# Other order of the recorded part, other layout of the experts' branches, few rows gathered early, the last full expert in groups of rows, and 22 unread products, in an attention–MLP–mixture-of-experts kernel

## The chip, the cores and the metric

One core of a Trainium2 chip runs the whole program. The metric is the device time of one execution in microseconds. TensorE is called PE, VectorE DVE, ScalarE ACT, GpSimd POOL and SyncE SP, as in the profile; "PEq", "SPq" and so on are the sequencers of these engines, which take the instructions in program order.

## The reference

Three blocks follow one another on 1152 tokens (two batches of 576) of width 512:

```python
# attention, 8 heads of 64, bias from the distance of two positions
x = (log1p(abs(i - j)) / log1p(max(i, 1)))[..., None]
bias = relu(x @ w1 + b1) @ w2
out = softmax(scale * q @ k.T + bias) @ v
# MLP, 512 -> 2048 -> 512
h = x @ w_in
y = (h * tanh(softplus(h))) @ w_out
# mixture of experts, top 1 of 8, capacity 288, 512 -> 1024 -> 512
e = argmax(y @ w_gate); gate = softmax(y @ w_gate)[e]
out[token] = gate * (relu(y[token] @ w1[e]) @ w2[e])   # the first 288 tokens of each expert
```

## The kernel before, in words

**The recorded part.** Attention, MLP and the routing are not written in the order in which they run. Each function records small operations (a product into one bank, an activation of one tile, one DMA) in a plan, and `emit` then walks the hand-written table `ORDER`: an entry is 8 times the number of the operation plus the number of its way, and the way picks the engine where an operation may run on more than one. The table alone sets what every engine and DMA queue finds in its row. The work goes in five tiles of 128 query rows: bias of the tile (matmuls at L518, activations at L507, a round trip of the bias row through memory, `bscr<-rbe` out and `ra<-bscr` back), scores (L619, L633), exponentials (L655), products with v (L727), then MLP in (L835) and out (L868, L872). L654 is DVE's first operation on the scores.

Matrices of the MLP and of the experts are split into a high and a low part in f16, and a product is three: high·high, high·low, low·high. L310 and L307 are DVE's and L1419 is ACT's instruction for such halves of a weight.

**The routing.** One-hot rows, counts (L1330) and slots give each expert its rows, at most 288 = 3 chunks of 96. The rows of the first expert are fetched by three indirect DMAs of POOL (L1144), split by ACT and DVE (L1149 is the low half), and turned by products with a 0/1 matrix (`first_slots`, L1173 and L1177; L1179 copies them out into `xT`). The last tile's tokens come from on-chip data; L1040 are sums of slots.

**The experts.** This part is plain code. `experts_list` sorts the experts by DVE; in this input three experts are full (`nf` = 3, more than 48 rows) and one has few rows (`nv` = 4). SP reads the sorted list into registers (L1595 to L1602), loads the next expert's first matrix (`load1`), the rows' table (`table`, L1396), and the second matrix (`load2`). `gemm1(k)` (L1434) makes 8 groups of 12 matmuls of 288 columns, `gemm2(k)` (L1467) 4 groups of 24, and behind each group transposes its result (`back`, L1453) and multiplies by the gate (L1454). `gather(k+1)` (L1402) fetches the next expert's rows and `xt` (L1424) turns them, inside `gemm2(k)`. `finish` ends with three scatters of 96 rows into `out` (L1448); in the loop it runs in the next expert's `gemm1`. The second matrix is split in `gemm1`, behind the groups 3 to 6 for k > 0 and behind 2 to 5 for the first expert.

`expert(k)` nests: `If(nf > k+1)` (L1572) the expert and the next one, `Else` (L1585) `If(nv > k+1)` `with_few(k)`, `Else` `last(k)`. All the `If` bodies of k = 0 to 6 lie first, and their `Else` bodies behind them from the innermost to the outermost, so the two conditions that end the experts' chain lead from L1572 of k = 2 over the code of four more experts to L1585. `with_few(2)` handles the last full expert together with the few rows (at most 48, in f32): loads of its matrices (`R1f`, `R2f`, L1505, L1507), `gemm1`, then the few rows' numbers and their gather (`xgf`, L1516), then `gemm2` with the few rows' products between the groups (`few_x` L1520, `few_h` L1525, `few_flip` L1533, `few_y` L1542), `finish`, the scaling of the few rows' result (L1560) and its scatter (L1561). `gemm2_last` exists in `before` too, for an input with no few rows: it makes the second product in 3 groups of 96 rows with 24 matmuls of 512 columns each, which need no transposing, and scatters each group as it is done.

Of the kernel before, what the change touches and what calls it, by code (L numbers as in the profile page):

```python
# [22 lines left out]
P = 128  # L23
# [15 lines left out]
    15464, 15472, 15480, 152, 184, 120, 128, 144, 136, 160, 168, 176, 104, 96, 112, 192, 0, 48, 200, 15488, 224, 208,  # L39
    216, 512, 56, 1328, 232, 4681, 1280, 616, 592, 608, 4672, 1416, 528, 816, 64, 673, 88, 72, 601, 648, 521, 4664,  # L40
    440, 537, 1337, 1344, 456, 449, 433, 4689, 624, 568, 544, 488, 697, 640, 689, 632, 464, 905, 656, 833, 4625, 480,
    496, 472, 825, 4433, 680, 1289, 1352, 1296, 888, 1304, 4544, 1360, 1432, 1312, 728, 4696, 664, 4425, 80, 1425,
    4561, 896, 1144, 240, 248, 1440, 840, 552, 1368, 1320, 560, 256, 576, 969, 504, 1376, 1192, 264, 1401, 4472, 777,
    1408, 584, 1160, 881, 1384, 1056, 848, 272, 864, 961, 856, 1208, 4488, 4536, 760, 1152, 704, 912, 4873, 4417, 872,
    1464, 712, 1008, 945, 4409, 4552, 4752, 1201, 952, 1216, 1392, 4568, 720, 4616, 1072, 1168, 1224, 928, 920, 753,
    4497, 4440, 736, 4609, 4857, 4601, 4481, 976, 4864, 280, 4880, 936, 8, 744, 1064, 2616, 769, 4632, 4504, 1016,
    4793, 992, 984, 4745, 784, 800, 792, 1480, 1176, 1080, 1448, 1000, 4809, 1473, 1088, 808, 1024, 2632, 4801, 4817,
    1488, 1032, 1496, 40, 1584, 1456, 4888, 1184, 4584, 1232, 4448, 4456, 4576, 1240, 2624, 1504, 1040, 1512, 1600,
    1592, 4824, 1096, 4592, 1608, 4464, 1248, 1720, 1728, 2128, 2120, 16, 1744, 1048, 4520, 4512, 1736, 4640, 1752,
    1264, 4528, 2640, 1521, 2648, 1624, 1632, 4649, 1648, 1784, 1800, 1256, 1816, 1616, 4656, 1104, 1640, 1792, 24,  # L50
    1656, 1760, 1664, 1552, 4896, 4904, 4912, 1680, 1528, 4736, 1272, 1672, 1808, 1824, 1768, 1560, 1536, 1696, 1688,
    1704, 1832, 1544, 1872, 4833, 1880, 1888, 1904, 1712, 2688, 4729, 1128, 4704, 1776, 4712, 4840, 4760, 1136, 1568,
    1976, 1984, 4848, 1840, 2000, 1896, 1920, 2656, 1912, 1112, 1936, 1952, 1864, 2760, 1992, 4776, 1944, 1928, 2008,
    1960, 2704, 1120, 2664, 2136, 2160, 2144, 2040, 2056, 2048, 2672, 2016, 288, 416, 1968, 2072, 2776, 4768, 2696,
    2232, 2024, 2080, 2064, 2680, 2088, 2712, 2168, 2152, 2032, 2256, 2264, 2192, 32, 4920, 2240, 2176, 2200, 2248,
    296, 2096, 2376, 2720, 2312, 2328, 2400, 2384, 2296, 2208, 2184, 2768, 2304, 2408, 2392, 2216, 2472, 2976, 4720,
    4784, 5456, 4944, 4936, 2448, 4928, 2336, 2728, 2992, 2784, 2432, 2416, 2480, 2272, 2496, 2985, 424, 2736, 2792,
    2280, 4960, 2440, 2488, 2288, 2504, 2512, 3000, 2552, 2568, 2424, 2536, 2744, 2456, 2520, 2800, 2752, 1576, 2320,
    2224, 2344, 2104, 2560, 1848, 2576, 4984, 2808, 4968, 2904, 4952, 3008, 1856, 2816, 4976, 4992, 2544, 2824, 2352,
    5056, 5032, 5016, 2584, 3016, 5000, 2912, 2464, 5080, 5064, 2920, 2528, 5024, 2112, 5216, 5040, 5008, 5072, 2360,  # L60
    5120, 5048, 2928, 3024, 2936, 2592, 3032, 2368, 2600, 5088, 3040, 5136, 5152, 2608, 2832, 2848, 3224, 3216, 2944,
    2952, 5144, 5128, 2960, 3408, 3616, 3416, 2840, 3624, 5240, 3232, 5160, 5224, 3312, 5232, 5248, 2968, 3048, 5272,
    5256, 5288, 2856, 3056, 3240, 5096, 2864, 3064, 3248, 3072, 7089, 2872, 2880, 3256, 3264, 3120, 3128, 5168, 3136,
    5280, 5296, 5264, 5312, 3080, 3144, 3088, 3424, 3152, 3160, 5320, 3304, 5336, 5208, 5200, 3168, 5328, 7153, 5104,
    3096, 3432, 5112, 3192, 5376, 3200, 5384, 4384, 5176, 5304, 3272, 3208, 3320, 3328, 3280, 3288, 3440, 3336, 5472,
    5496, 5480, 3448, 3456, 3512, 3520, 5568, 7105, 3344, 3464, 3296, 3352, 3472, 3360, 3368, 3392, 3400, 5504, 3528,
    5576, 5592, 5344, 5488, 3376, 10065, 3536, 5392, 5408, 5512, 3384, 5584, 5520, 3544, 7112, 5401, 3496, 312, 3552,
    376, 384, 5544, 5464, 3480, 408, 3488, 5552, 5352, 3632, 3560, 5600, 5632, 5641, 3504, 5528, 3640, 3600, 3608,
    5648, 3648, 3656, 5417, 3568, 3664, 7297, 5184, 5664, 3576, 3585, 5192, 3672, 3680, 2888, 4392, 4368, 5657, 2896,
    5673, 3832, 3824, 3105, 3720, 3728, 5360, 3177, 5369, 3592, 3689, 5536, 4376, 3736, 5424, 5432, 5712, 3704, 3696,  # L70
    5736, 5720, 7097, 7120, 7128, 5744, 7136, 5728, 3744, 3752, 5808, 5832, 3712, 5816, 7305, 3760, 5752, 3768, 7177,
    5824, 3936, 5784, 3816, 5872, 7544, 3184, 3112, 5793, 5768, 5840, 5760, 5776, 5440, 7161, 3840, 10321, 3928,
# [1588 lines left out]
```

## Time and profile before

| | us |
|---|---|
| median of 3 runs | 556.72 (555.08 to 559.42) |
| the profiled execution's own time | 556.07 |
| its span in the trace | 554.3 |
| PE busy | 492.3 (89%) |
| DVE busy | 442.0 (80%) |
| ACT busy | 389.3 (70%) |
| POOL busy | 36.6 (7%) |

The span is what the profiler recorded, first to last instruction; the execution's own time is 1.77 us longer. An engine's busy share is an average over stages: up to about 60 us the bias is made, from 60 to 415 attention and MLP run, from 415 to 431 the routing ends, and the three full experts and the few rows follow.

### The profile page before, as it was taken

To read this page: it belongs to the slowest core of one execution; us is meant where nothing else is said; L and a number is where in the kernel's file an instruction comes from. 1 tells how busy PE (TensorE), PEld (TensorE's weight loads), DVE (VectorE), ACT (ScalarE), POOL (GpSimd) and SP (SyncE) were. 2 spreads that over 40 slices of the span, in tenths; PEclk is the share of its full clock that TensorE was granted. 3 is DMA by queue.
4 is the path that set the end of the run, shared out by engine and by line. 5 is a ranking of instruction groups with operands and counts; after the bars stand their busy time and mean duration, and the time that the engine had idled before them with its cause. 6 is when DMAs were issued, how large, how long until landed. Compare 5 with 4: busy or idle time off the path is not lost.

```text
span 554.3 us, 11929 instructions
## 1 busy us (share of the span) xinstructions
PE 492.3 (89%) x4493; PEld 336.9 (61%) x4493; DVE 442.0 (80%) x1180; ACT 389.3 (70%) x803; POOL 36.6 (7%) x67
## 2 busy tenths in 40 slices
PE   5754987999999999999999999999994999977891
PEld 3311655865676754556787657995583677755460
DVE  7899999999889999999787857899878767747020
ACT  7999999989677999999876535577824377653110
POOL 1000100000000010000010000000012012202002
PEclk9786799999999999999999999999995899989797
DMA  8998775511000345257231023500002285871001
GB/s 324 381 360 300 263 279 195 209 60 60 24 2 31 133 138 195 86 178 242 81 98 38 0 83 129 178 1 2 19 23 63 89 293 153 243 284 37 8 4 43
DMA packets 28217, 73.85 MB, mean 133 GB/s; under 512 B 4838, under 2 KB 4966, under 8 KB 26096
## 3 DMA queue, kind: packets, MB, share of 16 engines
q1 hardware_dynamic: 26576, 69.21, 36.2%
q0 software_dynamic: 1568, 3.72, 2.3%
q8 instruction: 39, 0.64, 0.5%
q14 instruction: 34, 0.28, 0.2%
HBM read 55.27 MB, written 17.87 MB: 132 GB/s over the span
## 4 chain that ended last, share of the span: by engine, by line
PE 53%; DMA 16%; DVE 16%; issue 9%; ACT 4%; SPq 2%; POOL 0%; another core or an unknown queue 0%; POOLq 0%; ACTq 0%; DVEq 0%
PE pb L868 15%; PE pb L835 9%; DMA out<-OC,tid 8%; PE ps L835 5%; PE pb L727 5%; PE pb L518 4%; PE pb L663 3%; DVE rw L310 3%; DVE ra L654 3%; DMA bscr<-rbe 2%; PE ps L633 2%; PE ps L663 2%; PE pb L872 2%; ACT ra L507 1%; DVE ra L307 1%
## 5 line engine op out<-in xcount | busy, mean ns | idle before, releaser
L835 PEld LDWEIGHTS <-WIt 128*128 128x128 f16 x960 | 85.1, 98 | 9.9 <-issue 0.7
L835 PE MATMUL pb<-PX,WIt 128*128 128x256 f16 (+1 forms) x648 | 70.1, 265 | 0.0
L868 PE MATMUL pb<-WOt,ra 128*128 128x512 f16 x276 | 64.4, 379 | 0.1
L655 ACT ACTIVATE ra<-ra,rm 128x576 f32<-128x576 f32 x58 | 45.1, 779 | 10.7 <-DVE rm L654 10.3
L654 DVE CUSTOM_DVE_ANT_0 ra<-ps,ra 128x576 f32<-128x576 f32 x50 | 36.6, 752 | 9.5 <-PE ps L637 6.7
L868 PEld LDWEIGHTS <-ra 128*128 128x128 f16 x276 | 26.8, 98 | 28.1 <-issue 0.9
L507 ACT ACTIVATE ra<-AT,stab 128x320 f32<-128x320 f32 (+17 forms) x69 | 42.2, 645 | 1.5 <-DVE stab L307 1.4
L1467 PE MATMUL py<-HH,W 128*128 128x288 f16 x288 | 37.6, 286 | 1.6 <-DVE W L310 1.6
L1434 PEld LDWEIGHTS <-W 128*128 128x128 f16 x288 | 29.6, 103 | 14.0 <-issue 4.1
L727 PE MATMUL pb<-ra,AT 128*64 128x128 f32 (+1 forms) x640 | 37.0, 267 | 0.8 <-ACT ra L666 0.8
L518 PE MATMUL pb<-ra,w2s 128*32 128x512 f32 (+17 forms) x242 | 31.0, 520 | 6.0 <-ACT ra L507 3.5
L310 DVE SCALAR_TENSOR_TENSOR W<-AT,wsc,W 128x1024 f16<-128x1024 f32 x24 | 30.6, 1282 | 6.4 <-ACT W L1419 6.0
L727 PEld LDWEIGHTS pb<-ra,AT 128*64 128x64 f32 x640 | 32.1, 138 | 4.8 <-issue 2.3
L1467 PEld LDWEIGHTS <-W 128*128 128x128 f16 x288 | 28.0, 98 | 9.7 <-DVE W L310 2.2
L835 PE MATMUL ps<-PX,WIt 128*128 128x256 f16 (+1 forms) x312 | 31.1, 256 | 0.0
L310 DVE SCALAR_TENSOR_TENSOR rw<-rw 128x1024 int32<-128x1024 int32 (+1 forms) x25 | 29.8, 1195 | 0.0
L1054 POOL DMA_INDIRECT tbl<-pk,rm x9 | 10.9, 1211 | 273.3 <-DVE pk L1016 86.6
L532 ACT ACTIVATE rbe<-pb,rl 128x512 f32<-128x512 f32 (+47 forms) x57 | 25.7, 478 | 3.6 <-DMA bscr<-rbe 1.8
L619 PE MATMUL ps<-AT,rq 64*128 64x512 f32 x64 | 20.0, 703 | 8.2 <-DMA rq<-q 5.3
L663 PE MATMUL pb<-ident,ra 128*128 128x128 f32 x165 | 25.4, 283 | 1.7 <-ACT ra L655 0.9
L1434 PE MATMUL ph<-xT,W 128*128 128x288 f16 x144 | 22.4, 317 | 4.5 <-ACT jk L1206 3.9
L868 PE MATMUL pb<-WOt,rw 128*128 128x512 f16 x108 | 25.6, 379 | 0.0
(466 smaller groups left out, 1106.6 us busy)
## 6 DMA issues: line engine op xcount, KB each, us to landing
AT<-m SPq DMA_DIRECT2D x24, 512.0 KB
bscr<-rbe SPq DMA_DIRECT2D x36, 295.5 KB
ra<-bscr SPq DMA_DIRECT2D x29, 288.0 KB
rw<-wo SPq DMA_DIRECT2D x8, 1024.0 KB
rw<-wi SPq DMA_DIRECT2D x4, 1024.0 KB
WOt<-wi SPq DMA_DIRECT2D x4, 1024.0 KB
AT<-k SPq DMA_DIRECT2D x4, 576.0 KB
out<-ra SPq DMA_DIRECT2D x9, 256.0 KB
```

What stands on the lines that cost most here:

```text
L310: (eng or dve).scalar_tensor_tensor(out=out, in0=in0, scalar=s, in1=in1, op0=op0, op1=op1)
L507: on_act = lambda h_=h_, g=g: act.activation(h_.t[:, 0:dn], T[:, 0:dn], AF.Relu, bias=stab[:, g:g + 1])
L518: pe.matmul(ps.t[32 * c:32 * c + 32, 0:d1 - d0], w2s, hs[c].t[:, d0:d1], start=True, stop=True)
L532: op("ACT", c_act(n, 1, 50), lambda ends=ends: act.activation(*ends(), AF.Copy, scale=rl[:, blk:blk + 1]), r=[ps, "stab"], p=[be], alt=[(" ...
L654: op("DVE", c_dve(S), lambda i=i, own=own, m_=m_, b_=b_: dve.tensor_tensor_reduce(out=own(), in0=blk(s_.t[:, 960 * i:960 * i + S]), in1=bl ...
L655: op("ACT", c_act(S, 2), lambda i=i, m_=m_, col=col: act.activation(t_.t[:, S * i:S * i + S], t_.t[:, S * i:S * i + S], AF.Exp, bias=m_.t[ ...
L663: pe.transpose(pa.t[:, P * j:P * j + P], t_.t[:, 384 * n + P * j:384 * n + P * j + P], ident)
L727: pe.matmul(ov[64 * i:64 * i + 64, ct % 2, w * bb:w * bb + w], v_, t_.t[:, at + c0:at + c0 + w], start=n == 0, stop=n == 4)
L835: pe.matmul(ps.t[:, n * f_:n * f_ + n], WI[:, wv, ct, P * ft:P * ft + P], xt.t[:, xv, ct, 0:n], start=i == 0, stop=i == 11)
L868: pe.matmul(y_.t, gv()[:, g2, c:c + P], WO[:, wv, ft], **kw)
L1434: pe.matmul(ps[:, 0:SL], W1[:, wv, ct, P * ft:P * ft + P], XT[k % 2][:, xv, ct], start=i == 0, stop=i == 11)
L1467: pe.matmul(ps[:, 0:SL], W2[:, wv, ft, P * dt:P * dt + P], HH[:, hv, ft], start=ft == 0 and i == 0, stop=ft == 7 and i == 2)
```

## The change

Six edits. (1) `ORDER` is another permutation of nearly the same operations; it has one more. (2) That one is `unread` in `first_slots` (L1170 of the new kernel): 22 matmuls of 128x288 f16 into a bank that nobody reads, of data that are there by then, on PE in front of the first expert's row products. (3) `halves`: of the second matrix's four quarters ACT makes the high half of three, and DVE of the last; before it was two and two. (4) `gemm1` for k > 0: the row sums are reduced before the first group's low half, the size of the second matrix is found behind group 1, and its halves follow groups 2 to 5. (5) `with_few`: the few rows' gather stands before `gemm1`, `few_x` behind its seventh group, `gemm2_last` takes the place of `gemm2` and `finish`, with `few_h` and `few_flip` between its groups of rows and `few_y` at the end into another bank; the result goes to `XG[0]`, not to `OC[:, 0]`. (6) `expert`: for k below 2 as before, with the code in two functions; from k = 2 on the condition is turned, so that the end of the chain lies directly behind it and the next expert behind that.

```diff
@@ ORDER (every line differs) @@
-    15464, 15472, 15480, 152, 184, 120, 128, 144, 136, 160, 168, 176, 104, 96, 112, 192, 0, 48, 200, 15488, 224, 208,
...
+    136, 160, 104, 152, 120, 15472, 96, 128, 144, 15480, 168, 176, 112, 192, 0, 200, 184, 208, 216, 440, 888, 48, 224,
...
@@ first_slots @@
+        pz = pl.buf(RB)
+
+        def unread():
+            for i in range(22):
+                pe.matmul(pz.t[:, 0:SL], one, sl16, start=True, stop=True)
+        op("PE", 2600, unread, r=["sl1", "rc0", ("acc", 0), ("acc", 1)], w=[pz])
@@ halves @@
-        if i > 2 - m:
+        if i > 2:
@@ gemm1 @@
-            if k and ft == 2:
-                sized(k, 1, PO[0])
             act.activation(HH[:, 0, ft], ps[:, 0:SL], AF.Relu)
+            if k and ft == 0:
+                summed(k, 1)
             stt(HH[:, 1, ft], ps[:, 0:SL], 0.0, HH[:, 0, ft], ALU.max, ALU.subtract)
             if k and ft == 0:
                 finish(k - 1)
-                summed(k, 1)
-            if ft > 1 + bool(k) and ft < 6 + bool(k):
-                halves(k, 1, ft - 2 - bool(k))
+            if k and ft == 1:
+                sized(k, 1, PO[0])
+            if ft > 1 and ft < 6:
+                halves(k, 1, ft - 2)
             if k and more and ft > 3:
                 square(k + 1, 0, ft - 4, W["j"])
+            if between:
+                between(ft)
@@ gemm2_last @@
             act.activation(OC[:, c], ps, AF.Copy, scale=gat[:, c:c + 1])
             scatter(k, c)
+            if between:
+                between(c)
@@ with_few @@
         few_loads()
+        few_rows()
         if k:
-            gemm1(k, False)
-        few_rows()
-
-        def between(dt):
-            if dt == 0:
-                few_x()
-            if dt < 2:
-                few_h(dt)
-            if dt:
-                (few_flip if dt < 3 else few_y)((dt - 1) % 2)
-        gemm2(k, False, between)
-        finish(k)
+            gemm1(k, False, lambda ft: few_x() if ft == 6 else None)
+        else:
+            few_x()
+
+        def between(c):
+            if c < 2:
+                few_h(c)
+            if c:
+                few_flip(c - 1)
+        gemm2_last(k, between)
+        few_y(0)
         few_y(1)
-        act.activation(OC[:, 0], PH[0][:CS], AF.Copy, scale=sel[:, 0, 1:2])
+        act.activation(XG[0], PO[1][:CS], AF.Copy, scale=sel[:, 0, 1:2])
@@ expert @@
-        with tc.If(nf > k + 1) as more:
+        def next_():
...
-        with more.Else():
-            with tc.If(nv > k + 1) as more_:
+
+        def end():
+            with tc.If(nv > k + 1) as more:
                 with_few(k)
-            with more_.Else():
+            with more.Else():
                 last(k)
+
+        if k < 2:
+            with tc.If(nf > k + 1) as more:
+                next_()
+            with more.Else():
+                end()
+        else:
+            with tc.If(nf < k + 2) as done:
+                end()
+            with done.Else():
+                next_()
```

What stands in PE's row of instructions between the last product of the recorded attention/MLP part and the first row product of the first expert. Before (`ra_115` is the 0/1 matrix of the slots, `rw_105`, `rw_104` and `ra_109` are the high halves of the three gathered chunks):

```order
L1040 LDWEIGHTS U__150
L1040 MATMUL pb_140<-o_152,U__150 64x16
L1173 LDWEIGHTS rw_105
L1173 MATMUL pb_143<-ra_115,rw_105 128x96
L1173 LDWEIGHTS rw_104
L1173 MATMUL pb_143<-ra_115,rw_104 128x96
```

and in the changed kernel, where L1337 is the old L1330 and L1180 the old L1173:

```order
L1337 LDWEIGHTS one
L1337 MATMUL pb_144<-o_152,one 128x8
L1170 LDWEIGHTS one
L1170 MATMUL pb_142<-sl_173,one 128x288
...
L1180 LDWEIGHTS rw_106
L1180 MATMUL pb_142<-rw_105,rw_106 128x96
```

The pair at L1170 stands there 22 times, so PE passes through 22 loads and 22 products before it comes to the wait for the first expert's rows.

What stands in DVE's row at the end of the second full expert, where the chain of experts ends in this input. Before, the row behind the condition, which belongs to k = 3, and, 404 rows further on, the place to which the condition leads when it is not met:

```order
L1454 TENSOR_TENSOR OC<-po_5185,tb_5197 96x3x128
L1572 COMPARE_AND_BRANCH
L310 SCALAR_TENSOR_TENSOR HH<-ph_5181,HH 128x288
...
L1585 COMPARE_AND_BRANCH
L310 SCALAR_TENSOR_TENSOR HH<-ph_5181,HH 128x288
L1454 TENSOR_TENSOR OC<-po_5186,tb_5197 96x3x128
```

and in the changed kernel (L1606 and L1595 are the two conditions, `sel`, `tidf` and `gidf` the few rows' gate and numbers):

```order
L1465 TENSOR_TENSOR OC<-po_5219,tb_5231 96x3x128
L1606 COMPARE_AND_BRANCH
L1595 COMPARE_AND_BRANCH
L307 TENSOR_SCALAR sel<-tbf,hm 96x1 x4
L1522 TENSOR_TENSOR sel<-sel 96x2
L1523 CAST tidf<-sel 96x1
L307 TENSOR_SCALAR gidf<-sel 96x1
L327 TENSOR_REDUCE wsc<-wsc 128x1
L310 SCALAR_TENSOR_TENSOR HH<-ph_5215,HH 128x288
```

With three full experts and one of few rows both conditions now go on to the next row, and the few rows' numbers come first in it.

What stands in ACT's row from the last group of the last expert's `gemm1` to the end. Before (`YT` is a result still to be transposed, `XF`, `hs` and `HF` are the few rows):

```order
L1437 ACTIVATE HH<-pt_5188 128x288
L1468 ACTIVATE YT<-py_5183,wsc 128x288
L1521 COPY XF<-pt_5187 128x384
L1529 ACTIVATE hs<-ph_5181 96x512
L1468 ACTIVATE YT<-py_5184,wsc 128x288
L1538 COPY HF<-pt_5187 128x384
L1468 ACTIVATE YT<-py_5183,wsc 128x288
L1468 ACTIVATE YT<-py_5184,wsc 128x288
L1560 ACTIVATE OC<-ph_5181,sel 96x512
```

and in the changed kernel:

```order
L1530 COPY XF<-py_5218 128x384
L1443 ACTIVATE HH<-pt_5222 128x288
L1505 ACTIVATE OC<-py_5217,gat 96x512
L1538 ACTIVATE hs<-ph_5215 96x512
L1505 ACTIVATE OC<-py_5218,gat 96x512
L1547 COPY HF<-pt_5221 128x384
L1505 ACTIVATE OC<-po_5219,gat 96x512
L1569 ACTIVATE xg_5223<-po_5220,sel 96x512
```

The copy of the few rows has moved in front of the last group of `gemm1`, and three scaled copies that are scattered as they are take the place of four that PE still had to transpose.

## Rows read from the trace of the kernel before

**Rows 1.** The page: PE's busy tenths in 40 slices of 13.9 us

```profile
PE   5754987999999999999999999999994999977891
```

**Rows 2.** From 60 to 415: length, busy PE PEld DVE ACT POOL, PEclk, DMA share, GB/s

```profile
60.00:415.00 355.00, 347.59 (x3390) 242.36 (x3391) 314.95 (x876) 278.50 (x596) 12.89 (x32) 1.00 0.31 104
```

**Rows 3.** Chain that ended last, at 201 and at 288: start us, us, what

```profile
201.06 10.36 PE pb L868 x48
...
287.79 5.77 DMA ra<-bscr
```

**Rows 4.** PE, timeline 424 to 439: start us, us, what [idle before <-releaser]

```profile
424.98 0.34 PE L1173 MATMUL pb<-ra,rw 96*128 96x96 f16 x2 [5.33 <-DVE rw L1149]
...
430.90 5.05 PE L1434 MATMUL ph<-xT,W 128*128 128x288 f16 x24 [0.59 <-DVE xT L1179]
435.79 3.10 PE L1434 MATMUL pt<-xT,W 128*128 128x288 f16 x24
```

**Rows 5.** Two single microseconds, columns as in rows 2

```profile
418.00:419.00 1.00, 0.36 (x5) 0.26 (x5) 0.87 (x7) 0.16 (x1) 0.92 (x1) 0.50 0.46 131
...
435.00:436.00 1.00, 1.00 (x10) 0.80 (x9) 0.03 (x1) 0.01 (x1) 0.00 (x0) 1.00 0.00 0
```

**Rows 6.** Chain that ended last, at 449: the second expert's rows

```profile
448.68 6.07 DMA xg<-yscr,gid
```

**Rows 7.** PE, timeline 454 to 488

```profile
454.79 0.98 PE L1424 MATMUL pt<-ident,xg 96*128 96x96 f32 x8 [0.30 <-DMA xg<-yscr,gid]
...
459.69 1.78 PE L1434 MATMUL ph<-xT,W 128*128 128x288 f16 x12
...
472.58 2.61 PE L1467 MATMUL py<-HH,W 128*128 128x288 f16 x20
...
476.03 0.77 PE L1467 MATMUL py<-HH,W 128*128 128x288 f16 x4 [0.84 <-DVE W L310]
...
487.39 0.49 PE L1453 MATMUL po<-ident,YT 128*96 128x128 f32 x3
```

**Rows 8.** Conditions by sequencer: ns min/median/max, first to last start us

```profile
L1572 PEldq COMPARE_BRANCH  x3: 65/95/5960, 443.4 to 485.6; - x3
...
L1585 SPq COMPARE_BRANCH  x2: 34/36/38, 480.3 to 486.9; - x2
...
L1585 PEldq COMPARE_BRANCH  x2: 77/1657/3237, 491.6 to 535.8; - x2
```

**Rows 9.** DVE, timeline at 488: the last half of the last expert's first matrix

```profile
488.03 1.28 DVE L310 SCALAR_TENSOR_TENSOR W<-AT,wsc,W 128x1024 f16<-128x1024 f32 x1
```

**Rows 10.** PE, timeline 491 to 543

```profile
491.81 2.01 PE L1434 MATMUL ph<-xT,W 128*128 128x288 f16 x12 [3.93 <-ACT jk L1206]
...
505.79 2.61 PE L1467 MATMUL py<-HH,W 128*128 128x288 f16 x20
...
513.94 0.90 PE L1520 MATMUL pt<-ident,xgf 96*128 96x96 f32 x4 [3.99 <-DMA xgf<-yscr,gidf]
515.41 6.05 PE L1525 MATMUL ph<-R1f,XF 128*96 128x512 f32 x8 [0.57 <-ACT XF L1521]
...
524.56 3.60 PE L1525 MATMUL ph<-R1f,XF 128*96 128x512 f32 x8
528.00 0.49 PE L1533 MATMUL pt<-ident,hs 96*128 96x96 f32 x4
528.33 3.10 PE L1467 MATMUL py<-HH,W 128*128 128x288 f16 x24
...
538.96 3.60 PE L1542 MATMUL ph<-R2f,HF 128*96 128x512 f32 x8
```

**Rows 11.** Timelines of ACT and of POOL, from 510 to the end

```profile
542.91 0.68 ACT L1560 ACTIVATE OC<-ph,sel 96x512 f32<-96x512 f32 x1 [7.34 <-DMA out<-OC,tid]
...
510.69 0.94 POOL L1516 DMA_INDIRECT xgf<-yscr,gidf  x1 [7.02 <-DVE gidf L307]
...
549.52 0.92 POOL L1561 DMA_INDIRECT out<-OC,tidf  x1 [2.58 <-DMA out<-OC,tid]
```

More of the change, by code (lines that the diff above doesn't have):

```diff
@@ L1427, in tile_kernel, with gemm1 @@
     P3 = ((0, 0), (0, 1), (1, 0))
-    def gemm1(k, more=True):
+    def gemm1(k, more=True, between=None):
+        b_ = bool(k)
         for ft in range(8):
@@ L1454, in back, with gemm2 @@
         dve.tensor_tensor(out=OC[:, :, P * dt:P * dt + P], in0=po, in1=tb[k % 3][:, :, 1:2].bitcast(F32).to_broadcast([CS, NCH, P]), op=ALU.mult)
-    def gemm2(k, more=True, between=None):
-        if more:
-            if k == 0:
-                for i in range(4):
-                    square(1, 0, i, W["j"])
-            summed(k + 1, 0)
+    def gemm2(k):
+        if k == 0:
+            for i in range(4):
+                square(1, 0, i, W["j"])
+        summed(k + 1, 0)
         for dt in range(4):
@@ L1468, in gemm2 @@
             act.activation(YT[:, dt], ps[:, 0:SL], AF.Copy, scale=sca(k, 0, 7))
-            if more:
-                if dt == (k == 0):
-                    sized(k + 1, 0, PO[1])
-                if dt == 2:
-                    for c in range(NCH):
-                        xt(k + 1, c, (PT + PH)[c % 4])
-                if dt == 1 or dt == 2:
-                    halves(k + 1, 0, 2 * dt - 2)
-                    halves(k + 1, 0, 2 * dt - 1)
+            if dt == (k == 0):
+                sized(k + 1, 0, PO[1])
+            if dt == 2:
+                for c in range(NCH):
+                    xt(k + 1, c, (PT + PH)[c % 4])
+            if dt == 1 or dt == 2:
+                halves(k + 1, 0, 2 * dt - 2)
+                halves(k + 1, 0, 2 * dt - 1)
             if dt > 0:
                 back(k, dt - 1)
-            if more and dt > 1:
+            if dt > 1:
                 square(k + 1, 1, 2 * dt - 4, W["j"])
                 square(k + 1, 1, 2 * dt - 3, W["j"])
-            if between:
-                between(dt)
     def finish(k):
@@ L1519, in few_x @@
         for ct in range(4):
-            pe.transpose(PT[0][:, CS * ct:CS * ct + CS], xgf[:, P * ct:P * ct + P], ident[:CS, :CS])
-        act.copy(XF.rearrange("p c n -> p (c n)"), PT[0][:, 0:4 * CS])
+            pe.transpose(PY[1][:, CS * ct:CS * ct + CS], xgf[:, P * ct:P * ct + P], ident[:CS, :CS])
+        act.copy(XF.rearrange("p c n -> p (c n)"), PY[1][:, 0:4 * CS])
     def few_h(i):
```

6 lines of the change are left out of this document (3 added, 3 removed), and 216 rows, old and new, of the table ORDER.

## The prediction

> **What bounds the kernel now.** Read the page first: PE's 40 slices stand at 9 from 97 us to 416, fall to 4 in the slice from 416 to 430, and are loose from 485 to the end (7, 7, 8) [rows 1]. So there are three stages. From 60 to 415 us PE works 347.59 of 355 us at full clock [rows 2]: whatever is reordered there can win at most the 7.41 us that are left, and the chain of waits runs through PE itself, as in 48 matmuls of 512 columns in 10.36 us, 0.216 us each [rows 3]. The other two are the ones in which PE waits, and there the timeline of PE says for whom. Around 420 it stands 5.33 us, until the first expert's rows are there, and works on at half clock: the first 24 matmuls of L1434 take 5.05 us, the next 24 take 3.10 [rows 4]; in single microseconds the granted clock is 0.50 at 418 (1.2 GHz) and 1.00 (2.4 GHz) at 435 [rows 5]. From 488 on PE stands 3.93 us at the end of the experts' chain, later 0.84 and 3.99 us, and last there is a queue: POOL sends three scatters, each behind the landing of the one before, and a fourth for the few rows, at 549.52, when PE had ended at 538.96 + 3.60 = 542.56 [rows 7, 10, 11]. These are the places at which the change works.
>
> **The order of the recorded part.** The new table makes the same products. PE has 7.41 us of gaps to win from 60 to 415 [rows 2]; before 60 us it is fed by DMAs and by DVE, and the number of DVE's wide operations ahead of the first scores is nearly the same in both tables. I take 0. The bounds are about -5 us (two thirds of the gaps) and +6 us (one round trip of a bias row, 5.77 us [rows 3], that comes to stand bare).
>
> **The 22 products.** PE came to its wait at 424.98 - 5.33 = 419.65 [rows 4]. At half clock a matmul of 288 columns takes 5.05 / 24 = 0.21 us, at full clock 3.10 / 24 = 0.13. So 22 take 4.6 us if the clock is down and 2.8 if it is not: they fit into the 5.33 us and delay the rows' products by nothing, or by some tenths if PE comes later. What they can give is the clock. The row products and the first 24 of L1434 run at full clock if PE is kept busy: the 24 alone give 5.05 - 3.10 = 1.95 us, and the row products wait for copies anyhow. But PE then arrives 2 us earlier at the second expert's rows, and these do not come earlier: their gather stands on POOL behind SP's register loads and its load of the table, 448.68 + 6.07 = 454.75 [rows 6], and PE already waits 0.30 us for it [rows 7]. What the clock gives before comes back as a wait there, all but those 0.30 us, unless the lists on DVE end earlier too. I take -0.3; bounds -2.2 (the whole gain, if the lists move as well) and +2 (PE's longer wait lets the clock fall once more).
>
> **The second full expert.** The weight halves of its second matrix stand one group earlier and ACT takes one of DVE's; the stall of 0.84 us at 476.03 for the last half [rows 7] goes: -0.84. Against it, the few rows' 4 MB of weights are asked for earlier (next paragraph) and could lie on the gathers of the third expert's rows; bounds -0.84 and +0.9.
>
> **The end of the chain.** Before, PE's sequencer entered the condition at 485.6, took 5.96 us for it, and came to the next condition at 491.6; SP was through at 480.3 [rows 8]. The order shows that this is a jump over the code of four experts, and that both conditions now go on to the next row, so I take the 5.96 us away. What is late next: PE ends gemm2 at 487.88 - 0.84 - 0.3 = 486.74 [rows 7], and the last half of the first matrix ended on DVE at 488.03 + 1.28 = 489.31 [rows 9], some tenths to a microsecond earlier now. It is the eleventh of a group's 12 matmuls that needs it, 1.2 us in, so PE waits; I take 1.0 us, bounds 0.2 and 1.4. Then gemm1 takes 472.58 - 459.69 = 12.89 us as the second expert's did at full clock [rows 7], not 505.79 - 491.81 = 13.98 [rows 10], and `few_x` inside it half of its 0.90 us at half clock, 0.4. It ends at 486.74 + 1.0 + 12.89 + 0.4 = 501.0, against 505.79: -4.8, the two terms above in it. `few_x` finds its rows: the numbers are computed right behind the condition, at about 490, where the gather was issued at 510.69 before [rows 11], and 6 us later [rows 6] is 496, ahead of the seventh group's end at about 499.
>
> Here the Trainium skill has two rules. "Runtime: NRT & Kernel Launch", section Instruction fetch mechanics, says that a taken branch whose target lies outside the sequentially fetched window must fetch it before going on; the trace agrees for k = 2, with 5.96 us on PE against a median of 0.095. "Advanced Engine Details and Errata", section Control Flow Timing, gives about 108 ns for a compare-and-branch; by it the layout would be worth nothing, which this trace contradicts for a far target and bears out for the near ones (0.065 and 0.095).
>
> **The last expert's second half.** From there on, in the new order: 3 groups of 24 matmuls of 512 columns at 0.216 us, 15.5 us [rows 3]; two `few_h` and two `few_y` at 528.00 - 524.56 = 3.44 us each, 13.8 us; two flips at 528.33 - 528.00 = 0.33, 0.7 us [rows 10]. That is 30.0 us of PE without a wait: `xgf` is there, and the `few_h` that ran at half clock, 6.05 us for 3.60 [rows 10], follows no wait now. So PE ends at 531.0. The rest: 0.35 us to ACT's copy and 0.68 for it [rows 10, 11], an estimated 0.3 to POOL, and from POOL's issue to the end 554.3 - 549.52 = 4.78 [rows 11]. The three scatters of the full expert have gone out with their groups, over 5 us apart, so none is before the last one. End: 531.0 + 6.1 = 537.1, span before 554.3, -17.2 us in all; 12.4 of it lie behind gemm1: 1.0 is PE's wait at 509.19 and 4.0 at 513.94, some 3 the clock, 0.6 the wait for the copy, the rest the transposes and POOL's queue.
>
> **Sum.** 0 for the table, -4.8 to the end of gemm1, -12.4 behind it: the profiled execution's own 556.07 becomes 538.9. The median of the runs is 0.65 above it, less than what I can tell, so 538.9 stands.
>
> **Rivals.**
> (a) The stall stays. Two conditions in a row without a jump may still find their next rows unread. For it: PE's gap of 3.93 us sits at the condition, and a sequencer's cost there is seen only for a jump taken and for two that fell through cheaply [rows 8]; against it those two. The 3.93 and the 1.1 us of half clock come back, less the 1.0 us wait: 542.9.
> (b) The clock falls in PE's wait of 2 to 3 us at the second expert's rows: 24 matmuls lose 1.95 us: 540.9. For it: it had fallen with 5.33 us idle at 420; against: PE has been busy for 20 us by then.
> (c) The jump at the end. The end of the chain now lies in front of all other branches, and every engine leaves it by a jump over them. If POOL pays PE's price for a far jump, the 3.24 us that PE shows at its last branch, at 535.8 [rows 8], behind its last scatter: 542.1. Against it: POOL waits 2 us and more for that scatter's landing, and a sequencer can jump while it lands. The Runtime page's rule of the Trainium skill on far branches speaks for this rival.
> (d) The 22 products keep their 2 us, because SP's chain starts earlier too: 536.9.
> (e) The other side: the new table places the load of a bias row directly behind its store on SP's queue. Then every tile's scores wait for a round trip, 5.77 us [rows 3], with PE bare. Three of them, 17.3 us, eat up the whole gain, that is the point from which it decides; four, one per tile from the second on, make 23.1: 562.0. For it: one such wait stands in the chain now. Against it: PE's gaps from 60 to 415 sum to 7.41 us in the table of before [rows 2], and starts are alike in the new one.
>
> **How the numbers follow.** My forecast 0.52; (a) 0.10, (b) 0.11, (c) 0.10, (d) 0.09, (e) 0.03; 0.05 for a table that gains or costs 3 us or more otherwise. The likeliest time is 538.9. The table's bounds (-5, +6) are the widest of the unknown terms, and with (a) and (c) above and (d) below they give 531 to 548. About 1% is what a measurement of this kernel can tell from no change. Faster by over that needs less than 551.2; all cases but (e), a very costly table or two of (a), (c) together with it are below: 0.93. Within 1%: 0.04, slower: 0.03, both from (e) and the table.
>
> **What would show it.** In the profile of the changed kernel: conditions on all queues under 0.1 us near 480 to 490; PE's gap there about 1 us, for a weight half of DVE (a gap of 3 us or more with no engine's work before it is (a)); L1170's 22 products between 419 and 425; granted clock 1.00 in the first products of gemm1(0), and a wait of some 2 us for xg at the second expert's rows (none is (d)); no half clock behind gemm1 of the last expert; the third group of rows' scatter landed before the few rows'; POOL's last issue 4.8 us before the end (8 is (c)). The forecast is wrong if PE idles over 12 us from 60 to 415, or if PE's end is not near 531.

## The result, and the profile after

The changed kernel takes 542.42 us (541.07 to 545.01, 4 runs) against 557.25 for the one before in the same comparison: a ratio of 0.9739, 95% interval 0.9683 to 0.9796. The forecast of 538.9 had the sign and most of the size; 3.5 us of its gain are missing, and the wait for the third expert's rows was mis-sized. One run of experiment 4, of 1237.43 us, is left out of its median below.

The profiled execution took 543.5 us, its span is 541.6. The page, PE's busy tenths and its clock in 40 slices (13.5 us each now):

```profile
PE   4756988999999999999999999999998797979994
PEclk9896699999999999999999999999999898999998
```

The dip of [rows 1] at the first expert's rows is shallower (8 and 7 from 406 to 433 us, where a 4 stood), and the loose end is gone but for the last slice. New are the two 7s from 447 and from 474, in the midst of the experts. From 60 to 415 nothing has moved: PE's busy time by stage (columns as in [rows 2]) is 347.76 us where it was 347.59.

```profile
60.00:415.00 355.00, 347.76 (x3406) 243.10 (x3405) 311.13 (x885) 281.35 (x602) 13.52 (x33) 1.00 0.32 104
```

The timeline of PE from the unread products (L1170) to the end; start, us, what, and in brackets the idle time and who ended it:

```profile
417.50 4.52 PE L1170 MATMUL pb<-sl,one 128*128 128x288 f16 x22
423.53 0.20 PE L1180 MATMUL pb<-rw,rw 96*128 96x96 f16 x1 [1.51 <-DVE rw L1163]
...
429.50 3.12 PE L1442 MATMUL ph<-xT,W 128*128 128x288 f16 x24 [0.76 <-DVE xT L1186]
...
441.27 6.04 PE L1477 MATMUL py<-HH,W 128*128 128x288 f16 x48
...
453.48 0.55 PE L1431 MATMUL pt<-ident,xg 96*128 96x96 f32 x4 [2.11 <-DMA xg<-yscr,gid]
...
456.21 4.46 PE L1477 MATMUL py<-HH,W 128*128 128x288 f16 x24
...
460.84 1.63 PE L1442 MATMUL ph<-xT,W 128*128 128x288 f16 x12
...
473.15 3.10 PE L1477 MATMUL py<-HH,W 128*128 128x288 f16 x24
...
483.75 0.55 PE L1431 MATMUL pt<-ident,xg 96*128 96x96 f32 x4 [1.07 <-DMA xg<-yscr,gid]
485.21 0.55 PE L1431 MATMUL pt<-ident,xg 96*128 96x96 f32 x4 [0.90 <-DMA xg<-yscr,gid]
486.65 0.90 PE L1431 MATMUL ph<-ident,xg 96*128 96x96 f32 x4 [0.90 <-DMA xg<-yscr,gid]
...
487.99 3.95 PE L1477 MATMUL py<-HH,W 128*128 128x288 f16 x24
...
492.10 1.63 PE L1442 MATMUL ph<-xT,W 128*128 128x288 f16 x12
...
502.94 0.49 PE L1529 MATMUL py<-ident,xgf 96*128 96x96 f32 x4
...
504.74 5.34 PE L1504 MATMUL py<-W,HH 128*96 128x512 f16 x24
...
527.81 7.03 PE L1551 MATMUL po<-R2f,HF 128*96 128x512 f32 x16
```

Read it against [rows 4], [rows 7] and [rows 10], place by place:

| PE begins | before | after | difference |
|---|---|---|---|
| first expert, first matrix | 430.90 | 429.50 | -1.40 |
| second expert, first matrix | 459.69 | 460.84 | +1.15 |
| second expert, second matrix | 472.58 | 473.15 | +0.57 |
| third expert, first matrix | 491.81 | 492.10 | +0.29 |
| third expert, second matrix | 505.79 | 504.74 | -1.05 |
| PE's last product ends | 542.56 | 534.84 | -7.72 |
| POOL's last scatter is issued | 549.52 | 535.84 | -13.68 |
| end of the span | 554.3 | 541.6 | -12.7 |

Up to the third expert's second matrix nearly nothing is won; behind it everything. Each column is one execution, and the start of the second expert's first matrix alone differs by 3.9 us between kernels that are alike up to there (458.63 in experiment 1, 459.69 in the kernel before, 462.56 in experiment 2), so differences of 1 us show little; those from PE's end on are beyond that. In this pair two gains are taken back: PE is ahead when it comes to the second expert's rows and behind when it leaves them, and the second expert's second matrix takes 18.95 us to the start of the next expert's work (473.15 to 492.10), of which 2.87 are the three waits for the third expert's rows.

Single microseconds of the stretch, by the columns of [rows 2]; the granted clock stands behind POOL's busy time (1.00 is 2.4 GHz, 0.50 is 1.2 GHz):

```profile
422.00:423.00 1.00, 0.02 (x1) 0.10 (x1) 0.89 (x5) 0.00 (x0) 0.00 (x0) 1.00 0.03 1
426.00:427.00 1.00, 1.00 (x12) 0.82 (x10) 1.00 (x2) 0.00 (x0) 0.00 (x0) 0.50 0.13 47
456.00:457.00 1.00, 1.00 (x6) 0.67 (x5) 0.60 (x2) 1.00 (x2) 0.00 (x0) 0.50 0.68 262
487.00:488.00 1.00, 1.00 (x8) 0.92 (x7) 0.00 (x0) 0.41 (x2) 0.00 (x0) 0.50 1.00 383
```

Here is what two small waits cost beside themselves: behind the 2.11 us wait at 453 and the three waits before 487 the clock stands at 0.50, and the next 24 products take 4.46 and 3.95 us in place of 3.10. The DMA views show what runs beside the third expert's gathers. First the kernel before (476 to 486), then the changed one (474 to 490); the last column is the median time from issue to landing in us:

```profile
xg<-yscr,gid POOLq DMA_INDIRECT x3, 4.6
```

```profile
R1f<-m SPq DMA_DIRECT2D x4, 512.0 KB, 9.0
...
xg<-yscr,gid POOLq DMA_INDIRECT x3, 8.2
```

The same three gathers take 8.2 us instead of 4.6, beside the loads of the few rows' matrices. SP issues those 5.9 us earlier than before (481.55), 3.9 of them because it does not stall at the conditions any more: it passed from the first to the second from 476.4 to 480.3 before, and from 474.7 to 474.8 now. Their issue in SP's timeline:

```profile
475.68 2.19 SPq L1514 DMA_DIRECT2D R1f<-m  x4
```

The conditions at the end of the chain, by line as in [rows 8]: PE's is down from 5960 ns to 68, and SP is at the second one at 474.8:

```profile
L1595 SPq COMPARE_BRANCH  x2: 34/36/38, 474.8 to 481.6; - x2
...
L1606 PEldq COMPARE_BRANCH  x1: 68/68/68, 490.0 to 490.0; - x1
```

At the end, POOL's last issue in its timeline:

```profile
535.84 0.92 POOL L1570 DMA_INDIRECT out<-xg,tidf  x1 [6.28 <-ACT xg L1569]
```

and POOL's DRAIN instructions, the first of which comes next in POOL's row behind its last issue and branch, by line (shortest, median and longest ns, first to last start), of the changed kernel and then of the one before:

```profile
L1678 POOLq DRAIN  x3: 51/106/2503, 538.3 to 541.3; - x3
```

```profile
L1657 POOLq DRAIN  x3: 51/108/3723, 549.7 to 554.0; - x3
```

Before, POOL's first DRAIN starts at 549.7, 0.2 us behind the start of its issue at 549.52 [rows 11]; now it starts at 538.3, 2.5 us behind it, but the longest DRAIN is 1.2 us shorter. From the last issue to the end of the span it is 541.6 - 535.84 = 5.76 us instead of 4.78.

### The profile page after: what moved, and what is told of

Same layout as the page of the kernel before. It is cut to its first block, busy times and chain, and to the rows that moved or that the text cites. A ratio compares the mean times of both kernels' runs of the same rounds, so it can differ in the third digit from the quotient of the medians.

```text
span 541.6 us, 11894 instructions
## 1 busy us (share of the span) xinstructions
PE 495.9 (92%) x4479; PEld 336.9 (62%) x4479; DVE 434.3 (80%) x1172; ACT 394.8 (73%) x807; POOL 38.7 (7%) x67
## 4 chain that ended last, share of the span: by engine, by line
PE 57%; DMA 20%; DVE 11%; ACT 7%; issue 4%; SPq 1%; POOL 0%; another core or an unknown queue 0%; POOLq 0%; DVEq 0%; ACTq 0%
PE pb L868 15%; DMA xg<-yscr,gid 13%; PE pb L835 11%; PE pb L727 6%; PE ps L835 6%; DMA rw<-wi 4%; PE pb L663 3%; PE pb L518 3%; PE ps L633 3%; PE ps L663 2%; ACT ra L655 2%; ACT ra L666 2%; DVE WOt L310 1%; PE ps L619 1%; DMA out<-OC,tid 1%
## 5 line engine op out<-in xcount | busy, mean ns | idle before, releaser
L868 PE MATMUL pb<-WOt,ra 128*128 128x512 f16 x204 | 48.1, 379 | 0.0
L868 PE MATMUL pb<-WOt,rw 128*128 128x512 f16 x180 | 42.0, 379 | 0.0
L507 ACT ACTIVATE ra<-AT,stab 128x512 f32<-128x512 f32 (+17 forms) x62 | 38.6, 663 | 2.1 <-DVE stab L307 2.0
L1442 PEld LDWEIGHTS <-W 128*128 128x128 f16 x288 | 28.1, 98 | 7.8 <-DVE xT L1186 1.0
L868 PEld LDWEIGHTS <-rw 128*128 128x128 f16 x180 | 17.3, 98 | 20.5 <-issue 1.4
L532 ACT ACTIVATE rbe<-pb,rl 128x48 f32<-128x48 f32 (+25 forms) x64 | 28.6, 484 | 1.4 <-DMA bscr<-rbe 0.6
L310 DVE SCALAR_TENSOR_TENSOR rw<-rw 128x1024 int32<-128x1024 int32 x24 | 29.3, 1224 | 0.0
L1477 PE MATMUL py<-HH,W 128*128 128x288 f16 x192 | 26.9, 301 | 0.0
L666 ACT COPY ra<-pb 128x384 f32<-128x384 f32 x49 | 22.5, 492 | 3.5 <-PE pb L663 2.9
L307 DVE TENSOR_SCALAR ra<-AT,stab 128x544 f32<-128x544 f32 (+16 forms) x56 | 23.2, 445 | 0.9 <-PE pb L868 0.9
```

Source lines behind the costliest of these rows:

```text
L310: (eng or dve).scalar_tensor_tensor(out=out, in0=in0, scalar=s, in1=in1, op0=op0, op1=op1)
L507: on_act = lambda h_=h_, g=g: act.activation(h_.t[:, 0:dn], T[:, 0:dn], AF.Relu, bias=stab[:, g:g + 1])
L532: op("ACT", c_act(n, 1, 50), lambda ends=ends: act.activation(*ends(), AF.Copy, scale=rl[:, blk:blk + 1]), r=[ps, "stab"], p=[be], alt=[(" ...
L666: op("ACT", c_act(384, 0, 55), lambda dst=dst, src=src: act.copy(dst(), src()), r=[pa], w=[("tT", it, ct, b, n)], hold=[t_], alt=[("DVE", ...
L868: pe.matmul(y_.t, gv()[:, g2, c:c + P], WO[:, wv, ft], **kw)
L1442: pe.matmul(ps[:, 0:SL], W1[:, wv, ct, P * ft:P * ft + P], XT[k % 2][:, xv, ct], start=i == 0, stop=i == 11)
```

## The experiments

Each ratio is against the kernel before in the same comparison, whose median was 556.59 to 557.08 us.

**1. The layout alone.** Edit 6 in the kernel before.

```diff
-        with tc.If(nf > k + 1) as more:
...
+        if k < 2:
+            with tc.If(nf > k + 1) as more:
+                next_()
+            with more.Else():
+                end()
+        else:
+            with tc.If(nf < k + 2) as done:
+                end()
+            with done.Else():
+                next_()
```

> Only the branches' layout, in the kernel before. Theory 1: the 3.93 us gap at the end of the experts' chain and the half clock behind it go (about 5 us), but SP, without its own stall, sends the 4 MB of the few rows' weights about 6 us earlier, beside the gathers of the third expert's rows; PE then waits for these by 2.9 us and more in pieces, as in the changed kernel (1.07, 0.90 and 0.90 us), and loses clock: net -1 us, between -2.5 and +0.5; the gathers land about 8 us after issue instead of about 5. Theory 2 (the waits for the third expert's rows in the changed kernel have another cause): no such waits here, -4 to -5 us.

Measured: 557.03 us against 557.08, ratio 1.0004 (0.997 to 1.0037). PE's gap at the end of the chain is gone, and PE waits for rows instead; PE's waits from 415 on, in us, times and the longest (0.40 us of the first row are the second expert's, the rest the third's):

```profile
PE pt L1424 <- DMA xg<-yscr,gid: 4.0, 3, 3.0
...
PE ph L1424 <- DMA xg<-yscr,gid: 0.7, 1, 0.7
```

and the landing of the third expert's gathers (474 to 490):

```profile
xg<-yscr,gid POOLq DMA_INDIRECT x3, 8.9
```

and POOL's last issue in its timeline, 5.70 us before the end of the span at 554.7, where it was 4.78:

```profile
549.00 0.92 POOL L1561 DMA_INDIRECT out<-OC,tidf  x1 [2.58 <-DMA out<-OC,tid]
```

Theory 1 holds (0 lies within its -2.5 to +0.5): the layout removes a stall of some 4 us, brings a wait of about the same length and 0.9 us at the end, and is worth nothing that can be measured by itself.

**2. The few rows and the last expert alone.** Edit 5 in the kernel before (`gemm1` only gets the parameter `between`).

```diff
+        few_rows()
         if k:
-            gemm1(k, False)
+            gemm1(k, False, lambda ft: few_x() if ft == 6 else None)
...
-        gemm2(k, False, between)
-        finish(k)
+        gemm2_last(k, between)
+        few_y(0)
         few_y(1)
```

> Only the few rows and the last expert in groups of rows, in the kernel before (old order, old layout, old gemm1 schedule). By the forecast: from the end of the last gemm1 to the end of the span 36.1 us instead of 48.5, so -12 us (-12.4 and 0.4 for the copy inside gemm1). Rival: the gather of the few rows now stands in front of the scatters, or the weight halves come late for groups that need the whole second matrix in their first 5 us: -9 us or less, with a wait of PE inside the first group of 512 columns.

Measured: 545.59 us, ratio 0.9793 (0.9717 to 0.9869), -11.5 us. This edit is over three quarters of the gain of the change (11.5 of 14.8 us), and of the size that was worked out. In PE's timeline the gap at the condition is still there, without the layout:

```profile
495.15 2.94 PE L1434 MATMUL ph<-xT,W 128*128 128x288 f16 x12 [4.85 <-issue]
```

**3. The order and the unread products alone.** Edits 1 and 2 in the kernel before.

```diff
+        def unread():
+            for i in range(22):
+                pe.matmul(pz.t[:, 0:SL], one, sl16, start=True, stop=True)
...
```

> Only the new order and the 22 unread products, in the kernel before. Theory 1: PE reaches gemm1 of the first expert 1.4 us earlier and runs it at full clock (another 1.9 us), but the second expert's rows come as before, so PE waits there 2 to 3 us, its clock falls for about 3.4 us, and the second expert's gemm1 starts 0 to 1.5 us later than in the kernel before: 0 to +1.5 us in all. Theory 2 (the wait swallows the gain and no more): -0.5 to 0.

Measured: 556.81 us against 557.08, ratio 0.9988 (0.9959 to 1.0016): no difference that can be measured. The median fits theory 2 (-0.5 to 0), and the interval leaves theory 1's lower half open. PE's timeline has the wait that both speak of:

```profile
453.29 0.55 PE L1431 MATMUL pt<-ident,xg 96*128 96x96 f32 x4 [1.92 <-DMA xg<-yscr,gid]
```

**4. The changed kernel without the unread products.** Edit 2 undone, and its entry taken out of the table.

```diff
-        op("PE", 2600, unread, r=["sl1", "rc0", ("acc", 0), ("acc", 1)], w=[pz])
```

> The changed kernel without the 22 unread products. Theory 1 (they only move PE's wait to the second expert's rows and cost the clock there): the first 24 products of gemm1 of the first expert at half clock again, PE about 2 us later at the second expert's rows, a wait there under 1 us and no half clock: -2 to 0 us against the changed kernel. Theory 2 (they pay): +1 to +2 us against it.

Measured: 543.84 us (three runs, 542.72 to 545.48), ratio 0.9782 (0.9725 to 0.9838), which overlaps the changed kernel's interval: inconclusive from so few runs, and taken up again in 10. One thing it shows: its first 24 products of the first expert ran at full clock without the 22 ahead of them, though PE had stood for 5.90 us (PE's timeline):

```profile
422.51 0.24 PE L1065 MATMUL pb<-rw,rw 96*128 96x96 f16 x1 [5.90 <-DVE rw L1055]
...
428.60 3.11 PE L1327 MATMUL ph<-xT,W 128*128 128x288 f16 x24 [0.55 <-DVE A L199]
```

**5. The few rows' weights held back.** One tiny copy on SP's queue, behind the load of the few rows' table, reads the last piece of the third expert's turned rows; SP waits there until they are written, and the 4 MB go out behind it.

```diff
+    mark = dram.tile([1, 8], F16, name="mark")
...
-    def few_loads():
+    def few_loads(k):
         sp.dma_start(tbf, tv[bass.ds(evf[0], 1)].rearrange("o p c w -> (o p) c w"))
+        sp.dma_start(mark, XT[k % 2][0:1, 1, 3, SL - 8:SL])
...
```

> The changed kernel, with the few rows' 4 MB of weights held back on SP's queue behind a tiny copy that reads the last piece of the third expert's turned rows. Theory 1 (these weights beside the gathers make the third expert's rows late): the gathers land 5 us after issue instead of 8, the waits of 1.07, 0.90 and 0.90 us at the third expert's rows go, the clock stays at 1.00 between 486 and 490, the second product of the second expert takes 15 to 16 us instead of 19.1: -3 to -4 us against the changed kernel, 538.5 to 539.5. Theory 2 (it is POOL's queue: the gathers stand behind three scatters): the waits stay, no change, or slower by the weights that then come late for the first few_h.

Measured: 538.44 us (535.34 to 539.46), ratio 0.9667 (0.9622 to 0.9711). That is 4.0 us below the changed kernel's median, as theory 1 said, and although the intervals of the two ratios touch, its slowest run is faster than the fastest of experiment 6 in the same comparison (541.1), where the loads are not held. The profiled execution is its fastest, with a span of 533.6 us, and not all of its lead on the changed kernel's 541.6 is this edit's: at the second expert's first matrix, ahead of the edit, PE is 4.4 us earlier already (456.41). What the edit acts on is the stretch from the second expert's second matrix to the third's first: 13.96 us (469.30 to 483.26) in place of 18.95, where 15 to 16 were expected. In SP's timeline the loads now start at 482.10, when the third expert's rows have been turned:

```profile
481.54 0.31 SPq L1514 DMA_DIRECT2D mark<-xT  x1
482.10 2.18 SPq L1516 DMA_DIRECT2D R1f<-m  x4
```

By the DMA view (470 to 484) the gathers land in 4.2 us:

```profile
xg<-yscr,gid POOLq DMA_INDIRECT x3, 4.2
```

By PE's timeline it does not wait for them, there is no bracket:

```profile
478.67 0.83 PE L1432 MATMUL pt<-ident,xg 96*128 96x96 f32 x8
```

And the clock behind them, in the microsecond from 480, is 1.00:

```profile
480.00:481.00 1.00, 1.00 (x11) 0.80 (x9) 1.00 (x4) 1.00 (x3) 0.00 (x0) 1.00 0.00 0
```

**6. The second expert's table first.** SP loads it ahead of the first matrix's 2 MB.

```diff
+    table(1)
     for i in range(4):
         load1(1, i)
     gemm1(0)
...
-            table(k + 1)
+            if k:
+                table(k + 1)
```

> The changed kernel, with SP's load of the second expert's table of rows (2.2 KB) in front of the 2 MB of its first matrix instead of behind it. If the table's landing behind these 2 MB is what makes the second expert's rows late, POOL's gathers are issued at about 442 to 443 instead of 447.7, PE's waits at the second expert's rows (2.11, 0.35 and 0.26 us) and the half clock behind them go, and the second expert's gemm1 starts at 456 to 457 instead of 460.8: -3 to -4.5 us against the changed kernel. If the gathers were held by something else (DVE's row numbers, POOL), no change.

Measured: 542.73 us, ratio 0.976 (0.9713 to 0.9807): no gain that can be measured, although in the profile the mechanism is there. DVE computes the row numbers without a wait (in the changed kernel it waits 3.44 us for the table), the rows are gathered 2 us earlier, and PE does not wait at the second expert's rows. DVE's timeline:

```profile
444.46 0.17 DVE L307 TENSOR_SCALAR gid<-tb 96x3 uint32<-96x3 int32 x1
```

PE's timeline, the second expert's rows without a wait and the third's with the first of three:

```profile
452.38 1.06 PE L1431 MATMUL pt<-ident,xg 96*128 96x96 f32 x8
...
481.34 0.55 PE L1431 MATMUL pt<-ident,xg 96*128 96x96 f32 x4 [1.45 <-DMA xg<-yscr,gid]
```

The expected 3 to 4.5 us did not come. In this profile the second expert's first matrix starts at 457.36, 3.5 us earlier than in the changed kernel's, and from its second matrix to the third expert's first it takes 19.39 us in place of 18.95, so the second wait did not take them here; where they went this run does not show.

**7. Both.** Experiments 5 and 6 together.

> Both of the last two edits in the changed kernel. If the two waits are independent, the savings add up: -6 to -8 us against the changed kernel, about 535 us. If a wait removed in front only moves to the third expert's rows, which stand behind the first expert's scatters on POOL, only half of it: 538 to 539 us.

Measured: 538.18 us, ratio 0.9654 (0.9611 to 0.9697). The savings do not add up; the table in front gives nothing beyond holding the weights back. In this profile the second expert's gathers are issued at 444.72 instead of 447.72, but PE waits for them all the same (PE's timeline):

```profile
452.81 0.55 PE L1432 MATMUL pt<-ident,xg 96*128 96x96 f32 x4 [0.59 <-DMA xg<-yscr,gid]
454.65 0.80 PE L1432 MATMUL ph<-ident,xg 96*128 96x96 f32 x4 [1.28 <-DMA xg<-yscr,gid]
```

By the DMA view (440 to 456) they land in 6.9 us, where the changed kernel's land in 5.4:

```profile
xg<-yscr,gid POOLq DMA_INDIRECT x3, 6.9
```

SP issues the 2 MB of the second expert's second matrix from 441.66 on (441.90 in the changed kernel), so the earlier gathers lie nearer to these loads. That is the pattern of the third expert's rows; no run holds these loads back, so here it is not shown as the cause.

**8. The third expert's rows ahead of the scatters.** As 7, with the third expert's table and gathers before the second expert's `gemm1`.

```diff
             if k:
+                table(k + 1)
                 for i in range(4):
                     load1(k + 1, i)
+                gather(k + 1)
                 gemm1(k)
...
```

> As the last one, and the third expert's table and gathers also in front of the second expert's gemm1, so ahead of the first expert's scatters on POOL. The gathers then land long before they are needed, PE waits for no rows at all: another -0.5 to -2 us against both edits, about 534 us. Rival: the scatters, now behind the gathers, hold DVE's and ACT's buffers: no change.

Measured: 537.9 us, ratio 0.9668 (0.9622 to 0.9715): no change against 5 or 7. No wait for the third expert's rows was left to take away.

**9. The changed kernel with the old layout.** Edit 6 undone.

> The changed kernel with the old layout of the branches. Theory 1 (the layout takes a stall of the sequencers away and puts the late third expert's rows in its place): PE has its gap of 4 to 5 us at the end of the chain again and no waits for the third expert's rows, so no difference from the changed kernel beyond 1 us, 541.5 to 543.5. Theory 2 (in the changed kernel, where PE is earlier, the layout pays): +2 to +5 us, 544.5 to 547.5.

Measured: 542.94 us, ratio 0.9751 (0.9714 to 0.9788): the changed kernel's time, as theory 1 said. In PE's timeline the stall is back, and the third expert's rows cost 0.51 us in place of 2.87:

```profile
482.51 0.55 PE L1431 MATMUL ph<-ident,xg 96*128 96x96 f32 x4 [0.51 <-DMA xg<-yscr,gid]
...
491.16 2.38 PE L1442 MATMUL ph<-xT,W 128*128 128x288 f16 x12 [4.50 <-issue]
```

The gathers land in 5.7 us (DMA view, 474 to 490):

```profile
xg<-yscr,gid POOLq DMA_INDIRECT x3, 5.7
```

From POOL's last issue, in its timeline, to the end of the span it is 541.1 - 536.56 = 4.54 us:

```profile
536.56 0.92 POOL L1570 DMA_INDIRECT out<-xg,tidf  x1 [6.28 <-ACT xg L1569]
```

**10. Held back, without the unread products.** Experiments 4 and 5 together.

> The changed kernel with the weights held back, without the 22 unread products, against the one with them and held back (538.44 us). If the products give back what they win by a longer wait at the second expert's rows: within 1 us of it. If they pay when nothing behind takes it back: +1.5 to +2 us.

Measured: 538.82 us, ratio 0.9684 (0.9647 to 0.9722), 0.4 us from experiment 5: the 22 products give nothing that can be measured, though the two intervals leave room for 2 us.

**11. The schedule of the weight halves alone.** Edits 3 and 4 in the kernel before.

```diff
-        if i > 2 - m:
+        if i > 2:
...
-            if ft > 1 + bool(k) and ft < 6 + bool(k):
-                halves(k, 1, ft - 2 - bool(k))
+            if ft > 1 and ft < 6:
+                halves(k, 1, ft - 2)
```

> Only the new schedule of the weight halves inside gemm1 (edits 3 and 4), in the kernel before. The two stalls of 0.8 us at L1467 (476.03 and 509.19) go; at the second, PE then waits as long for the few rows' gather, which comes later: -0.8 us. Rival: the first is given back in front of the third expert's rows: 0.

Measured: 553.71 us, ratio 0.9944 (0.9921 to 0.9967), -3.1 us, more than either side of the expectation. Both stalls for a weight half are gone, and PE's wait for the few rows did not grow by that but shrank, from 3.99 us; PE's timeline:

```profile
511.49 0.62 PE L1524 MATMUL pt<-ident,xgf 96*128 96x96 f32 x4 [3.11 <-DMA xgf<-yscr,gidf]
```

and POOL's:

```profile
508.28 0.94 POOL L1520 DMA_INDIRECT xgf<-yscr,gidf  x1 [3.13 <-DVE gidf L307]
```

The gather of the few rows is issued at 508.28 instead of 510.69 [rows 11]: in the kernel before, its numbers stood on DVE behind the last weight halves. The expectation had left DVE's queue out. In the changed kernel the numbers come before `gemm1`, so this part cannot be won twice.

**12. The few rows, the layout and the held-back weights alone.** Edits 5 and 6 and experiment 5 in the kernel before.

> The kernel before with the few rows' edit, the new layout and the held-back weights, but the old order, the old gemm1 schedule and no unread products. If the order, the products and the schedule give nothing that lasts: within 1.5 us of the changed kernel with held-back weights (538.44). If they give 1 us each: 540.5 to 541.5.

Measured: 539.4 us, ratio 0.9693 (0.9655 to 0.973): within 1 us of experiment 5, which has the new order, the unread products and the new schedule besides. Against experiment 2 (545.59) layout and held loads together give 6.2 us. No run holds the loads in the old layout, so the share of each is not measured.

The waits for the third expert's rows in all fourteen profiles say the same: 2.87 to 4.25 us in the four with the new layout and free loads (the changed kernel and experiments 1, 4 and 6), 0 to 0.51 in the five with the old layout, and none in the five with held loads.

## Why the forecast was right, and where not

**The last expert's second half: right.** From the end of `gemm1` PE was to work 30.0 us without a wait; it worked from 504.74 to 534.84, 30.1. Experiment 2 gave the whole edit 11.5 us where 12.4 less 0.4 were forecast. The few rows were there for `few_x` with no wait, and no product behind ran at half clock. Among the parts that the forecast named for this gain, PE's wait at 509.19 was misread: it is 0.79 us and not 1.0, which changes no term of the sum.

```profile
509.19 0.77 PE L1467 MATMUL py<-HH,W 128*128 128x288 f16 x4 [0.79 <-DVE W L310]
```

**The order of the recorded part: right at 0.** PE's 7.41 us of gaps from 60 to 415 are 7.24 now; with the unread products the new order moved nothing measurable (experiment 3). Rival (e) did not come.

**The 22 products: the size not contradicted, the reason not borne out.** -0.3 was taken; experiments 3 and 10 find no difference, with intervals that leave room for 1 us and more to either side. But the products do not hold the clock, as the step assumed. In the kernel before the clock stood at 0.50 at 418 already [rows 5], ahead of the wait that began at 419.65, so that wait did not take it. In the changed kernel's profile the products ran at half clock themselves (4.52 us for 22; 2.85 in experiment 3, at full clock), PE then stood 1.51 us, and the row products ran at 0.50 again. The first 24 products of the first expert took between 3.11 us and 5.39 (experiment 6) in the seven profiled kernels that have the 22 products, and between 3.11 and 5.05 in the seven that do not. What decides the clock there stays open; these products alone do not.

**The second full expert: the stall went as forecast.** At 473.15 all 24 products of the first group run without a wait.

**The second expert's rows: rival (b) came in the profile, but not as the change's doing.** PE waited 2.11, 0.35 and 0.26 us, the clock stood at 0.50 behind it, and the lead of 1.4 us at the start of the first expert became a lag of 1.15. But PE waits there in kernels without the 22 products too: 1.90 us in experiment 4, 1.75 in experiment 10, 3.89 in experiment 2 with its old order, against 0.30 in the kernel before and 0 in experiment 5. The wait differs from one execution to the next, and what sets it stays open.

**The end of the chain: the step that failed.** The forecast took -4.8 us to the end of `gemm1`; the trace shows -1.05, and the layout by itself is worth nothing (experiments 1 and 9). That the stall would go was right, 5960 ns to 68. The wait of 1.0 us for a weight half that was put in its place did not come: there is no bracket at 492.10. What failed is "Against it, the few rows' 4 MB of weights are asked for earlier ... and could lie on the gathers of the third expert's rows", which stood in the paragraph on the second expert with a bound of +0.9. It measured 2.87 us of waits and a stretch at half clock, and experiment 5 gives it back as 4.0 us. The stall had been SP's too, and had kept these loads off the gathers without anyone meaning it. With that term at 4 the sum would have been 538.9 + 4 = 542.9. By the forecast's own sign it shows: PE's end was to be near 531 and is 534.84. The held-back kernel's 538.44 comes to the forecast's number, but partly by chance: the wait of 1.0 us is not there, and the end costs 1.0 us more than was forecast.

**The number alone would have misled.** 542.42 lies nearer to rival (a)'s 542.9 and rival (c)'s 542.1 than to the forecast, and neither came as told: the stall is gone, and the end costs a third of (c). The upper bound of the range is not the sum of the terms that it names: 538.9 + 6 + 4.0 + 3.2 is 552.1, not 548.

**The end of the program: rival (c) in a third of its size.** From POOL's last issue to the end it is 5.76 us in the changed kernel, 541.6 - 535.84, and 4.54 with the old layout (experiment 9). It is the layout that does it: all nine profiles with the new one have 5.65 to 6.15, all five with the old one 4.50 to 4.78. POOL's DRAIN, which begins 2.3 us later behind its issue than before, fits a jump to the end that lies there. The Trainium skill's "Runtime: NRT & Kernel Launch", section Instruction fetch mechanics, says that a taken branch out of the fetched window has to fetch its target first; the 1.0 us on the 4.78 of before is in line with that, but no row here shows the fetch itself.

## What to carry to other kernels

A stall on an engine that issues loads is also a delay of these loads: before taking it away, list what this engine sends next and what lands at that time. Small indirect transfers on which PE waits should land before bulk loads that are needed 20 us later go out; one copy that reads the last row as it is written held the bulk back here at no price. Moving them earlier need not help: in experiment 7 they came to lie nearer to other loads and landed later behind their issue. A gain of PE in front of rows that do not come as much earlier turns into a wait for them (PE came 3.1 us earlier to the second expert's rows, and their gathers were issued 1.0 us earlier), and such a wait of 2 to 3 us can cost clock beside itself. And a place in one profile that differs by 4 us between kernels alike up to there is not to be explained by an edit; medians, or the same sign in many profiles, are.

## What had not been expected of the hardware

Three gathers of 96 rows each land in 8.2 to 9.1 us (median of the three) where the issue of 4 MB of loads begins with them (the changed kernel and experiments 1, 4 and 6), in 4.5 to 5.7 where it begins some 4 us behind the first (4.35 in the kernel before; experiments 2, 3, 9 and 11), and in 3.7 to 5.5 where the loads are held (experiments 5, 7, 10 and 12). Whether it is the DMA engines or the memory that they share, no run tells. A matmul stream behind an idle time of PE comes out at either clock in programs whose code ahead of it is the same: 5.05 us for 24 products in the kernel before and 4.92 in experiment 1, 3.11 in experiment 2, where the recorded part is unchanged and PE had stood 5.54 us.
